# A sequence-DFT regrouped: four rows on one partition, odd halves turned by per-partition tangents, 95-column products

## The chip, the cores and the metric

The kernel runs on one core of a Trainium2 chip. The metric is the device time of one execution in microseconds (us). Every time in this study comes from an execution that was recorded as being in the fast state, at a mean granted TensorE clock of 0.99 or more. The kernel before takes 1940.77 us (median of three runs, 1940.24 to 1942.61).

Engine names as the profile uses them: PE is the matrix engine, PEld its weight loads, DVE the vector engine, ACT the scalar engine, POOL the GpSimd engine. SBUF is the large on-chip memory, PSUM the accumulator memory of PE.

## The reference

```python
# x: (8, 3008, 256); w_in: (256, 2048); w_out: (2048, 256); all float32
X = np.fft.fft(x, axis=1)              # along the sequence, 3008 points
X = np.fft.fft(X, axis=2)              # along the 256 channels
x = X.real.reshape(24064, 256)
h = x @ w_in
g = h * np.cos(h)
out = g @ w_out
```

The kernel doesn't transform the channels as such: the channel DFT is linear, so it is folded into `w_in` once. Because only the real part is wanted, one column of products serves two rows of the result, as a sum and as a difference (h_plus and h_minus), so 12032 columns are enough. What stays are two jobs. One is the "s-DFT", a 3008-point transform along the sequence for each of the 8 batches, which fills two rings of columns, `Rr` (real) and `Ir` (imaginary). The other is the dense part, 376 steps that read the rings.

## The kernel before

The program is one long list of events, each with a time in units of a step `T`. Each of the four busy engines works in the order of that list, so an event placed in a slot must be done before whatever follows it there. This is the dense step (lines joined and regrouped; `ACT`, `DVE`, `POOL` and `PE` added as remarks):

```python
for i in range(total):                 # total = 376 steps, 8 to a tile
    for dt, fn in (
        (-1.9, ext),                   # ACT: writes the 129th channel's share into the PSUM bank H
        (0.0, mm_P),                   # PE: H += Wc x Rr     (2 products of 256 columns)
        (0.9, dbl),                    # ACT: E = 2 H
        (2.17, mm_Q),                  # PE: H += Ws x Ir     (2 products)
        (3.55, h_minus),               # DVE: G[0:512] = E - H
        (4.2, k_plus), (4.8, k_minus), # ACT: round to integers
        (T + 0.2, r_plus), (T + 0.9, r_minus),     # DVE: H - round(H), in turns
        (T + 1.5, sin_plus), (T + 2.21, sin_minus),# ACT: the cosines
        (T + 2.2, g_plus), (T + 2.9, g_minus),     # DVE: h cos h
        (T + 2.91, sum_1), (T + 3.6, sum_3), (T + 4.4, sum_2), (2 * T + 0.3, sum_4),  # POOL
        (2 * T + 0.87, mm_X1), (2 * T + 3.04, mm_X2),  # PE: 7 products with w_out
    ): at(i * T + dt, ...)
```

Eleven products of 256 columns a step, two fp32 records each, keep PE busy. DVE has two gaps a step, after `h_minus` and after `r_minus`; POOL has one, after `sum_4`. Into these gaps goes the preparation of the next batch: POOL folds the loaded rows `xl` into even and odd halves (`e`, `o`), PE multiplies the halves with cosine and sine matrices `MC`, ACT and DVE unfold the result into the rings.

```python
class Dft:                             # one half transform (real or imaginary, even or odd k) of one batch
    def first_part(self):  self.mms(0, self.uv, False)    # for even k: 4 products of 189 or 190 columns
    def second_part(self): self.mms(1, self.pb, False)    # for even k: 3 products of 188 to 377 columns
    ...
def at_dft(step, gap, b, ri, kodd, stat):
    at(t + 2.905, lambda: d().clear())        # DVE: memset of a PSUM bank
    at(t + 4.75, lambda: d().first_part())    # PE
    at(t + T + 1.46, lambda: d().side())      # ACT
    at(u + 1.01, lambda: d().unfold())        # DVE
    at(u + 2.95, lambda: d().seed())          # ACT
    at(u + 4.75, lambda: d().second_part())   # PE
    at(u + T + 1.01, lambda: d().minus_sum()) # DVE, in0 from SBUF, in1 from PSUM
    at(u + T + 1.46, lambda: d().plus_sum())  # ACT
```

Each fp32 product gives two records in the trace. There are 33 such half transforms, 4 for each of 8 batches and one for a first channel column.

## Time and profile before

| | before |
|---|---|
| time | 1940.77 us (1940.24 to 1942.61) |
| span of the profiled run, mean granted clock | 1939.9 us, 0.999 |
| PE time lost against the widths of its products (own count) | 19.2 us |
| of that up to the first step / in steps 0 to 20 / later | 6.0 / 5.8 / 7.4 us |
| first step's products start | 36.3 us |
| s-DFT records, sum of their start-to-start spacings | 462, 95.3 us |

The profile's end of a matmul is modelled, so a busy share of 99% doesn't say that PE works without gaps. The own counts in this document go from the start of one PE record to the start of the next. A 256-column record, when nothing holds it, is 0.216 us after the one before; what exceeds the free spacing is called lost. For narrow and early records the free spacing is a choice, so another count differs by some us. (The Trainium skill, "Perfetto Trace Analysis", "Identifying the Most-Contended Engine", says the same of the matmul row: not a good measure, since pipelined instructions look smaller.)

The first table and the chain of waits, with three groups, from the page of the kernel before. A group's columns are line, engine, operation, output and input, shapes, count, then busy us and mean ns of one, then the engine's idle time just before it and what ended most of that.

```profile
PE 1921.9 (99%) x8878; PEld 1657.6 (85%) x8878; DVE 1426.7 (74%) x2387; ACT 1478.6 (76%) x2854; POOL 1412.0 (73%) x1926
...
PE 95%; DVE 2%; ACT 1%; issue 1%; DMA 1%; POOL 0%; SPq 0%; DVEq 0%; POOLq 0%
...
L293 POOL TENSOR_TENSOR G<-G 128x256 f32<-128x256 f32 x1500 | 1076.6, 728 | 491.8 <-DVE G L787 426.7
...
L284 PE MATMUL H<-Rr,Wc 128*128 128x256 f32 x1504 | 387.2, 380 | 0.7 <-ACT H L296 0.3
...
L284 PE MATMUL pB<-G,WT 128*128 128x256 f32 x752 | 224.0, 379 | 1.0 <-POOL G L293 1.0
```

PE is the bottleneck and hardly waits: 0.7 us in 1504 first products, 1.0 us for POOL's sums. The list of waits of the kernel before (us in all, times, longest):

```profile
POOL G L293 <- DVE G L787: 426.7, 333, 4.5
DVE G L787 <- ACT G L296: 256.4, 274, 4.2
...
ACT G L296 <- DVE G L290: 181.2, 357, 2.1
```

One step of the kernel before, from its timeline (start us, length us, what, how many; in brackets the idle time before). Only DVE's two first operations of the step and POOL are shown:

```profile
1011.15 3.02 POOL L293 TENSOR_TENSOR G<-G 128x256 f32<-128x256 f32 x4 [0.63 <-DVE G L787]
1011.52 0.68 DVE L290 TENSOR_TENSOR G<-E,H 128x512 f32<-128x512 f32 x1
...
1012.87 0.69 DVE L290 TENSOR_TENSOR G<-H,G 128x512 f32<-128x512 f32 x1 [0.66 <-ACT G L296]
...
1014.13 1.00 POOL L349 TENSOR_TENSOR e<-xl 128x381 f32<-128x381 f32 x1
```

Keep two things of it. POOL's four sums run without a break for 3.02 us, just where DVE has its gap, from 1012.2 (the end of `h_minus`, the `G<-E,H` line) to 1012.87. And `r_plus`, the `G<-H,G` line, starts 1.35 us after `h_minus`.

### The profile page before, as it was taken

To read this page: it belongs to the slowest core of one execution; us is meant where nothing else is said; L and a number is where in the kernel's file an instruction comes from. 1 tells how busy PE (TensorE), PEld (TensorE's weight loads), DVE (VectorE), ACT (ScalarE), POOL (GpSimd) and SP (SyncE) were. 2 spreads that over 40 slices of the span, in tenths; PEclk is the share of its full clock that TensorE was granted. 3 is DMA by queue.
4 is the path that set the end of the run, shared out by engine and by line. 5 is a ranking of instruction groups with operands and counts; after the bars stand their busy time and mean duration, and the time that the engine had idled before them with its cause. 6 is when DMAs were issued, how large, how long until landed. Compare 5 with 4: busy or idle time off the path is not lost.

```text
span 1939.9 us, 28429 instructions
## 1 busy us (share of the span) xinstructions
PE 1921.9 (99%) x8878; PEld 1657.6 (85%) x8878; DVE 1426.7 (74%) x2387; ACT 1478.6 (76%) x2854; POOL 1412.0 (73%) x1926
## 2 busy tenths in 40 slices
PE   8999999999999999999999999999999999999998
PEld 4888888888888888888888888888888888888887
DVE  5687777777777767777777777777767777677777
ACT  3777778877788777877778877787778777777786
POOL 6878768877687767877678776778768886555654
PEclk9999999999999999999999999999999999999999
DMA  9611210102101031110310103011030110000101
GB/s 274 35 29 17 61 47 20 18 14 71 33 20 18 11 78 31 18 20 9 87 27 13 22 7 94 13 21 26 7 84 15 24 27 7 17 12 12 21 10 25
DMA packets 258994, 67.59 MB, mean 35 GB/s; under 512 B 239970, under 2 KB 250858, under 8 KB 258842
## 3 DMA queue, kind: packets, MB, share of 16 engines
q1 hardware_dynamic: 251994, 50.81, 14.0%
q0 software_dynamic: 4672, 14.69, 2.6%
q8 instruction: 71, 1.16, 0.3%
q14 instruction: 81, 0.66, 0.1%
q10 hardware_dynamic: 2176, 0.26, 0.1%
HBM read 40.98 MB, written 24.69 MB: 34 GB/s over the span
## 4 chain that ended last, share of the span: by engine, by line
PE 95%; DVE 2%; ACT 1%; issue 1%; DMA 1%; POOL 0%; SPq 0%; DVEq 0%; POOLq 0%
PE H L284 38%; PE pC L284 17%; PE pD L284 16%; PE pB L284 16%; PE pA L284 8%; DMA w<-in_moe_w_in_dram 1%; DVE G L787 1%; ACT G L296 1%; DVE G L290 0%; ACT E L296 0%; DVE M L290 0%; DVE v L290 0%; DVE ab L290 0%; DVE ot L900 0%; DVE u L290 0%
## 5 line engine op out<-in xcount | busy, mean ns | idle before, releaser
L293 POOL TENSOR_TENSOR G<-G 128x256 f32<-128x256 f32 x1500 | 1076.6, 728 | 491.8 <-DVE G L787 426.7
L787 DVE SCALAR_TENSOR_TENSOR G<-H,G 128x512 f32<-128x512 f32 x376 | 259.2, 689 | 256.7 <-ACT G L296 256.4
L290 DVE TENSOR_TENSOR G<-H,G 128x512 f32<-128x512 f32 x376 | 260.0, 692 | 220.5 <-ACT G L296 217.5
L296 ACT ACTIVATE E<-H 128x512 f32<-128x512 f32 x376 | 224.4, 597 | 216.9 <-PE H L284 213.3
L284 PE MATMUL pC<-G,WT 128*128 128x256 f32 x1504 | 387.3, 379 | 2.1 <-DVE u L290 1.8
L284 PE MATMUL H<-Rr,Wc 128*128 128x256 f32 x1504 | 387.2, 380 | 0.7 <-ACT H L296 0.3
L284 PE MATMUL H<-Ir,Ws 127*128 127x256 f32 x1504 | 386.7, 378 | 0.7 <-ACT E L296 0.7
L296 ACT ACTIVATE H<-Rb,wex 128x256 f32<-128x256 f32 x752 | 360.6, 480 | 22.4 <-DVE G L787 8.1
L296 ACT ACTIVATE G<-H 128x512 int32<-128x512 f32 x376 | 224.5, 597 | 181.8 <-DVE G L290 180.6
L284 PEld LDWEIGHTS H<-Rr,Wc 128*128 128x128 f32 x1504 | 283.5, 190 | 48.5 <-ACT H L296 2.6
L284 PEld LDWEIGHTS pC<-G,WT 128*128 128x128 f32 x1504 | 283.7, 189 | 45.9 <-PE H L284 5.0
L284 PEld LDWEIGHTS H<-Ir,Ws 127*128 127x128 f32 x1504 | 284.7, 189 | 41.9 <-ACT E L296 1.4
L296 ACT ACTIVATE G<-G,halfpi 128x512 f32<-128x512 f32 x376 | 269.4, 717 | 0.6 <-DVE G L290 0.6
L290 DVE TENSOR_TENSOR M<-G,M 128x512 f32<-128x512 f32 x376 | 257.7, 685 | 0.0
L290 DVE TENSOR_TENSOR G<-E,H 128x512 f32<-128x512 f32 x376 | 255.5, 679 | 0.1
L787 DVE SCALAR_TENSOR_TENSOR G<-G,M 128x512 f32<-128x512 f32 x376 | 254.6, 677 | 0.6 <-ACT M L296 0.5
L296 ACT ACTIVATE M<-M,halfpi 128x512 f32<-128x512 f32 x376 | 246.1, 654 | 0.4 <-DVE M L290 0.3
L284 PE MATMUL pB<-G,WT 128*128 128x256 f32 x752 | 224.0, 379 | 1.0 <-POOL G L293 1.0
L296 ACT ACTIVATE M<-G 128x512 int32<-128x512 f32 x376 | 224.4, 597 | 0.0
L284 PE MATMUL pA<-G,w 128*128 128x256 f32 x752 | 223.8, 379 | 0.3 <-DVE G L787 0.3
L284 PE MATMUL pD<-G,WT 128*128 128x256 f32 x752 | 223.8, 379 | 0.0
L284 PE MATMUL pD<-G,w 128*128 128x256 f32 x752 | 223.7, 379 | 0.0
(147 smaller groups left out, 1886.6 us busy)
## 6 DMA issues: line engine op xcount, KB each, us to landing
out_dram<-ot SPq DMA_DIRECT2D x496, 32.0 KB
xl<-in_x_dram SPq DMA_DIRECT2D x32, 256.0 KB
out_dram<-ot SPq DMA_DIRECT2D x256, 2.0 KB
xl<-in_x_dram SPq DMA_DIRECT2D x31, 128.0 KB
Rb<-r SPq DMA_DIRECT2D x10, 376.0 KB
w<-in_moe_w_in_dram SPq DMA_DIRECT2D x4, 512.0 KB
w<-in_moe_w_out_dram SPq DMA_DIRECT2D x1, 2048.0 KB
MC<-dft_mats SPq DMA_DIRECT2D x2, 942.0 KB
```

The costliest lines, as they stand in the source:

```text
L284: nc.tensor.matmul(out_, lhsT=lhsT, rhs=rhs, start=start, stop=stop, skip_group_check=True)
L290: pin(nc.vector.tensor_tensor(out=o, in0=a, in1=b, op=op))
L293: pin(nc.gpsimd.tensor_tensor(out=o, in0=a, in1=b, op=op))
L296: pin(nc.scalar.activation(out=o, in_=i, func=func, **kw))
L787: nc.vector.scalar_tensor_tensor(out=o, in0=h, scalar=TWO_PI, in1=c, op0=ALU.mult, op1=ALU.mult)
```

## The change

Its intent is to cut PE's work in the s-DFT. Before, a half transform took its rows in six groups on up to 128 partitions and streamed 1514 or 1884 columns in 14 records through PE. Now rows s, 376-s, 376+s and 752-s lie on one partition (96 partitions, 8 slots), so that the cosine and sine sums can be split further, and a half transform needs 16 records of 94 or 95 columns. The price: for the odd halves, and with four steps each for a part of the even ones, the pairs of rows have to be turned by an angle that depends on the row. That is done in lifting steps, each `p + t q` with one tangent (or another constant) per partition from the table `RC`. The core of the diff, cut (`...`) and with comments added:

```diff
+    def stt(o, i, n, add):              # one turning step, on DVE, both inputs in SBUF
+        pin(nc.vector.scalar_tensor_tensor(
+                out=o, in0=i, scalar=RC[:, n : n + 1], in1=add, op0=ALU.mult, op1=ALU.add))
+    def turns0(z, ri):                  # 4 steps of 128 elements, for even k
...
+    def turns1(v, ri):                  # 16 steps, for odd k; both for real and imaginary: 40 a batch
...
     def dft_parts(ri, kodd, par):
-        ... four products of nh = 190 or 189, then two or three of up to 377 columns
+        ... four products of 95, 94, 95, 95 (or 95, 94, 95, 94) columns for each parity
...
+    def odd(self, down):                # the odd columns are now sums of two SBUF tiles, on DVE
+        for k0, step, n, a, b, op in sums(self.kodd):
+            ... vtt(self.ring[0:M, sl], u, v, op)
...
-        at(u + 1.01, lambda: d().unfold())
-        at(u + 2.95, lambda: d().seed())
+    def dve_room(n):                    # how much of a DVE gap may be filled, in us
+        return 0.0 if step % 8 in (...) else 0.64      # 0.72 in the first nine steps
+    def on_dve(n, cost, fn):            # next gap with room for cost
+    def dve_ns(elements):
+        return max(0.2, 0.08 + 1.04e-3 * elements)
+    def turn_all(n, ops, cost=0.19):    # a turning step is planned at 0.19 us
...
+    at(3 * T + 1.46, flip_ext)          # ACT: reads a slow load of the 129th channel
```

The folds on POOL go from 128 partitions x 381 elements to 96 x 508. The unfolding loses its two DVE passes and gets 16 such odd sums a batch instead.

## The prediction

> **What bounds it now.** The page's first table gives PE 99% (1921.9 of 1939.9 us), ACT 76%, DVE 74%, POOL 73%; the chain of waits is 95% PE. Matmul ends are modelled, so I counted start to start: the eleven 256-column products of a step run at 0.216 us a record, two records a product, without gaps. Against widths, PE loses some 19 us, 8 of them before 48 us and 4 more before 145 us; later there is next to no idle to recover. Only less PE work or a shorter prologue helps.
>
> **What PE sheds.** The s-DFT now is 462 records (14 of 188 to 377 columns a transform, 33 transforms). Their spacing follows columns (0.160 us at 190, 0.316 at 376); together 95.3 us. The change streams 758 or 756 columns a transform instead of 1514 or 1884, but in 16 records of about 95 columns: 528 records. By columns that would be 528 x 0.079 = 42 us. I don't believe it: the 16-column products that turn the extra channel, with 128-column weights, are spaced 0.118 us in the trace of before. So weight loading is the floor, and it doesn't shrink with 96 rows (those loads have 32). The Trainium skill, "TensorE: Matmul & The Clock Gate", LDWEIGHTS section, says that columns, not rows, set the load (128/1.2 = 107 ns); the trace's 118 agrees roughly. So 528 x 0.118 = 62 us: PE sheds about 33 us, not 53. The extra-channel work is about even.
>
> **What the others get.** POOL folds: before about 16 x 765 elements a batch at 2.35 ns (a 381-element piece takes 0.997 us), 36 us; after about 19,300 elements, 49 us: +80 us in all, to about 80%. DVE: 40 tangent turns and 16 odd sums a batch at 0.19 to 0.28 us, less the unfolds: +8 us a batch, to about 78%. ACT even. The new DVE ops read two SBUF operands. In the trace of before such an op (the v<-v,p sum) stretches an overlapping POOL fold from 0.997 to 1.46 us, as the skill's "SBUF — State Buffer", Terms, says of the shared port pair (the loser blocks). A fold piece also grows to about 1.3 us. The POOL sum that releases the pB product now ends a median 1.1 us early (5th percentile 0.5), so most of this hides; I allow 5 us of new PE stalls.
>
> **Prologue.** The first step's products start at 36.3 us. DVE folds of the first batch grow by a third (762 to 1016 elements, about 0.87 to 1.14 us), and halves and turns come before the first transform: it starts near 29 to 30 instead of 24.9 us. Given back: two odd folds become accumulating DMAs, and constants shrink by about 2.7 MB. Net +2 us.
>
> **Sum.** 1940.8 - 33 + 5 + 2 = about 1914 us (-1.4%). Range 1904 to 1930. Chances: faster by over 2% 0.11, within 2% 0.86, slower 0.03.
>
> **What would show it.** Spacing of the new records: 0.118 us (right), 0.08 (columns bind; then nearer 1895), or 0.16 and more. Sum of the s-DFT spacings about 62 us. First step's start at 37 to 41 us. PE's waits on POOL's and DVE's G in the list of waits: from about 2 us to 5 to 10. POOL near 80%, fold pieces often over 1.5 us where turns overlap.
>
> **What would make it wrong.** Narrow records cheaper than 0.118; POOL delayed past the 1.1 us margin in many steps (tenths of a us over 376 steps are tens of us); accumulating DMAs that land late and hold the first imaginary transform; PSUM banks held too long by the two-step transforms.

## The result, and the profile after

The changed kernel takes 2000.93 us (median of 4 runs, 1999.21 to 2002.8) against 1941.69 us (1940.24 to 1943.31) for the kernel before in the same rounds. Ratio 1.0305, 95% interval 1.0287 to 1.0323: slower by 3%. A ratio here is the mean time of one kernel's fast runs over that of the other's of the same rounds, so not quite the ratio of the medians that are quoted. The result is right (the output agrees with the reference).

The same lines of the page, for the changed kernel:

```profile
PE 1923.4 (96%) x8944; PEld 1627.1 (81%) x8944; DVE 1662.0 (83%) x2797; ACT 1486.4 (74%) x2861; POOL 1495.5 (75%) x1908
...
PE 70%; DVE 19%; ACT 4%; issue 3%; DMA 3%; SPq 1%; POOL 0%; DVEq 0%; POOLq 0%; ACTq 0%
...
L298 POOL TENSOR_TENSOR G<-G 128x256 f32<-128x256 f32 x1500 | 1082.5, 732 | 457.6 <-DVE G L796 355.3
L289 PE MATMUL H<-Rr,Wc 128*128 128x256 f32 x1504 | 395.4, 385 | 23.1 <-ACT H L301 23.1
...
L289 PE MATMUL pB<-G,WT 128*128 128x256 f32 x752 | 230.2, 388 | 6.0 <-POOL G L298 4.8
```

PE's busy time even rose by 1.5 us. That is the trap of the modelled ends: start to start, the s-DFT fell from 95.3 us in 462 records to 63.1 us in 528 (the page's count of PE goes up by the same 66), and PE's lost time rose from 19.2 to 106.7 us. Those two, -32.2 and +87.5, give +55.3 us, which is nearly the whole difference of the spans, 1997.4 - 1939.9 = 57.5 us. A recount that takes the median spacing of each shape as free gives 24.8 and 118.5 us lost (+93.7), and 94.3 and 58.9 us for the s-DFT when nothing holds it (-35.4), +58.3 us together. So some 4 of the 63.1 us are stalls inside the s-DFT.

DVE is the engine that grew: +235 us, where I had expected some 65 (8 a batch), and its share of the chain went from 2% to 19%. Its new groups, with shapes kept apart (turning steps of two tiles, then one of the odd sums):

```profile
L423 DVE SCALAR_TENSOR_TENSOR e<-e,RC 96x128 f32<-96x128 f32 x128 | 74.5, 629 | 0.0
L423 DVE SCALAR_TENSOR_TENSOR o<-o,RC 96x127 f32<-96x127 f32 x128 | 71.7, 607 | 0.0
...
L295 DVE TENSOR_TENSOR Ir<-sb 127x188 f32<-127x188 f32 x14 | 10.3, 774 | 0.0
```

A turning step of 128 elements takes 0.61 to 0.63 us on average, not the 0.19 that the change plans with. Where POOL isn't running it takes 0.34 us (own selection from the trace); four in a row, while POOL computes nothing, take 1.13 us, 0.28 each. So the 0.19 was too little even without POOL, and the larger part of the excess is what happens beside POOL. In all, 344 steps that read `RC` take 209.6 us and 152 odd sums 87.6 us.

The waits that grew in the changed kernel's list:

```profile
POOL G L298 <- DVE G L796: 355.3, 309, 4.5
ACT G L301 <- DVE G L295: 284.8, 445, 2.2
...
PEld pB L289 <- POOL G L298: 26.7, 60, 2.3
...
PE H L289 <- ACT H L301: 23.1, 27, 7.7
...
PE H L289 <- DVE H L556: 12.6, 11, 1.4
...
ACT x L301 <- DMA x<-in_x_dram: 10.3, 1, 10.3
```

ACT waits 104 us more for DVE's `G`; PE now waits for ACT's write of H, for DVE's clearing of the DFT bank and for POOL's sums. The timeline of a step in which a real odd half is turned shows how that starts:

```profile
1020.62 3.03 POOL L298 TENSOR_TENSOR G<-G 128x256 f32<-128x256 f32 x4 [0.55 <-DVE G L796]
...
1020.99 0.68 DVE L295 TENSOR_TENSOR G<-E,H 128x512 f32<-128x512 f32 x1
...
1021.58 2.21 DVE L423 SCALAR_TENSOR_TENSOR e<-e,RC 96x128 f32<-96x128 f32 x3
...
1023.72 0.68 DVE L295 TENSOR_TENSOR G<-H,G 128x512 f32<-128x512 f32 x1
...
1024.43 0.72 ACT L301 ACTIVATE G<-G,halfpi 128x512 f32<-128x512 f32 x1 [0.95 <-DVE G L295]
```

Three turning steps, planned at 0.57 us, take 2.21 us, as long as three of POOL's sums, and the last ends 0.14 us after POOL's last sum (1023.79 and 1023.65). `r_plus` comes 2.73 us after `h_minus` instead of 1.35, and ACT sits idle for it. `h_minus` itself runs in its usual 0.68 us in the middle of POOL's sums: it has one input in PSUM. Over the whole trace, a turning step that starts while a POOL sum is running ends 0.147 us (median) after the end of that sum; one that comes just as a sum starts takes 0.88 us, that is 0.73 + 0.15. Of the 320 steps of 127 or 128 elements, 209 take more than 0.4 us (0.78 on average). The reverse is rare: 8 steps began 0.04 to 0.08 us before a sum; they kept their 0.33 to 0.34 us, and the sum took 0.84 to 0.89 us instead of 0.73.

At the start there are two more losses. The chain of waits of the changed kernel up to 75 us contains a load that lands at 71.5 us:

```profile
32.15 39.31 DMA x<-in_x_dram
...
71.55 0.13 ACT x L301
```

ACT works in order and waited there 10.3 us (the last of the waits above), in step 3 of 376; from step 3's first products to step 4's, PE took 14.7 us (59.6 to 74.3) instead of 4.75. And the first products start later, by the timelines of before (first two lines) and after:

```profile
24.90 1.56 PE L284 MATMUL pA<-MC,e 128*128 128x190 f32 x8
...
36.34 1.13 PE L284 MATMUL H<-Rr,Wc 128*128 128x256 f32 x4 [0.26 <-issue]
```

```profile
31.42 0.68 PE L289 MATMUL pA<-MC,e 95*128 95x95 f32 x4 [0.76 <-DVE e L362]
...
43.49 1.13 PE L289 MATMUL H<-Rr,Wc 128*128 128x256 f32 x4 [1.74 <-ACT H L301]
```

### The profile page after: what moved, and what is told of

Same layout as the page of the kernel before. It is cut to its first block, busy times and chain, and to the rows that moved or that the text cites. A ratio compares the mean times of both kernels' runs of the same rounds, so it can differ in the third digit from the quotient of the medians.

```text
span 1997.4 us, 28934 instructions
## 1 busy us (share of the span) xinstructions
PE 1923.4 (96%) x8944; PEld 1627.1 (81%) x8944; DVE 1662.0 (83%) x2797; ACT 1486.4 (74%) x2861; POOL 1495.5 (75%) x1908
## 4 chain that ended last, share of the span: by engine, by line
PE 70%; DVE 19%; ACT 4%; issue 3%; DMA 3%; SPq 1%; POOL 0%; DVEq 0%; POOLq 0%; ACTq 0%
PE H L289 27%; PE pB L289 12%; PE pC L289 12%; PE pD L289 12%; PE pA L289 6%; DVE G L295 5%; DVE G L796 4%; DVE M L295 2%; ACT G L301 2%; DMA x<-in_x_dram 2%; DVE o L423 2%; DVE e L423 2%; DVE v L295 1%; DMA xl<-in_x_dram 1%; ACT M L301 1%
## 5 line engine op out<-in xcount | busy, mean ns | idle before, releaser
L289 PE MATMUL H<-Rr,Wc 128*128 128x256 f32 x1504 | 395.4, 385 | 23.1 <-ACT H L301 23.1
L289 PEld LDWEIGHTS H<-Rr,Wc 128*128 128x128 f32 x1504 | 277.0, 191 | 74.5 <-ACT H L301 37.7
L289 PE MATMUL pB<-G,WT 128*128 128x256 f32 x752 | 230.2, 388 | 6.0 <-POOL G L298 4.8
L289 PE MATMUL pB<-G,w 128*128 128x256 f32 x752 | 225.1, 381 | 0.3 <-DVE u L295 0.2
```

The source lines that it names most:

```text
L289: nc.tensor.matmul(out_, lhsT=lhsT, rhs=rhs, start=start, stop=stop, skip_group_check=True)
```

## The experiments

The theory after the first look: DVE's new operations have two inputs in SBUF, and such an operation has to wait for the POOL operation that is running. (The Trainium skill has the lock: "SBUF — State Buffer", Terms, on the shared port pair, "the loser **fully blocks**, it doesn't share bandwidth", and "GPSIMD Engine Reference", Specifications, lists the conflict with DVE instructions that have two SBUF inputs.) The rivals: the mere number and time of the new DVE operations; the one slow load; the longer start; too many banks taken by the two-part transforms. The last two have no run of their own; e2 leaves the banks as they are.

Seven kernels were run, each timed in 4 runs.

### e1: the read of the slow load put three steps later

```diff
-    at(3 * T + 1.46, flip_ext)
+    at(6 * T + 1.46, flip_ext)
```

> The changed kernel with one edit: the ACT copy that flips the extra channel's rows is issued at step 6, not step 3. Theory A (ACT executes in order and sits 10.3 us behind the slow one-channel load, so steps 3 to 4 take 14.7 us): the wait of ACT on the x load goes to under 1 us, the step from 3 to 4 falls to about 5 us, time about 1990 us (10 less than 2001). Rival: the stall in the first 100 us is DVE work that only moves elsewhere: time within 3 us of 2001.

Measured: 1990.93 us (1989.31 to 1994.38), ratio 1.0248 (1.0231 to 1.0265); right result. So this edit takes back 10 of the 59 us. From step 3's first products to step 4's, PE now takes 6.7 us (own reading of the trace), a little more than the 5 expected. Its list of waits no longer has the load; ACT's wait for DVE stays on top:

```profile
ACT G L301 <- DVE G L295: 288.1, 445, 2.2
```

The slow load is a real, separate cause, and the smaller one.

### e2: the wide turning steps replaced by operations with one input (wrong result)

```diff
     def stt(o, i, n, add):
+        if o.shape[1] >= 127:
+            pin(nc.vector.transpose(out=o[:, 0:96], in_=i[:, 0:96]))
+            return
```

As many DVE operations, in the same places, writing the same tiles (96 columns of them), but each reading one. The 24 narrow turning steps of the 129th channel stay.

> The changed kernel with wrong results on purpose: every tangent turn of 127 or 128 columns becomes a 32-block transpose of 96 columns of its first operand on DVE, so the same number of DVE instructions in the same places, but one SBUF input instead of two. Theory L (a two-SBUF-input DVE op cannot start while POOL executes one; it waits for POOL's op to end, 0.73 us for a sum): turns fall from a mean of 0.6 us to about 0.25 us, DVE busy falls by some 100 us, PE stalls of 106 us are about halved, time 1940 to 1970 us. Rival C (the count and place of inserted DVE instructions is what delays the chain): time stays within 5 us of 2001. Rival P (POOL's longer fold pieces delay its sums): stays within 10 us of 2001.

Measured: 1953.27 us (1948.11 to 1955.75), ratio 1.0048 (1.0031 to 1.0065), relative error 1.12 as intended. 48 us are gone. Its first table and the group that took the turning steps' place:

```profile
PE 1903.4 (97%) x8944; PEld 1636.6 (84%) x8944; DVE 1550.4 (79%) x2797; ACT 1486.7 (76%) x2861; POOL 1493.9 (76%) x1908
```

```profile
L423 DVE STREAM_TRANSPOSE e<-e 96x96 f32<-96x96 f32 x128 | 25.5, 244 | 0.0
```

The number of operations is not the cause, and neither is the number of banks, which is the same here. But their time changed together with their inputs, 0.24 us against 0.62, and the data flow isn't the real one. So the next pair puts the same question to the other kernel.

### b1 and b2: the same DVE traffic in the kernel before, with two inputs and with one

Both add 360 operations whose result nobody reads, in bursts of three every third step, at the place in the step where the change puts its turning steps. The sources are constants.

```diff
+    for i in range(10, total - 8, 3):
+        for _ in range(3):
+            at(i * T + 4.25, lambda: vtt(sd, CC[0:96, 0:128], CC[0:96, 128:256], ALU.add))      # b1
+            at(i * T + 4.25, lambda: pin(nc.vector.transpose(out=sd, in_=CC[0:96, 0:128])))     # b2
```

> The kernel before, with 360 idle-value DVE additions of 96x128 of two SBUF operands into a scratch tile, three in a burst after the h_minus of every third step, where POOL is in its sums. Theory L: each takes about 0.6 to 0.9 us instead of 0.25, a burst takes about 2.2 us in an idle window of 0.66 us, and the time rises by 40 to 150 us. Rival C: the rise is the same as for the one-input control below.

> Control to the one above: the same 360 places, but 32-block transposes of 96x128 with one SBUF operand. Theory L: each takes about 0.25 to 0.3 us, the time rises by under 8 us. Rival C: the same rise as with pairs.

Measured: b1 2007.69 us (2004.69 to 2008.17), ratio 1.0332 (1.0315 to 1.0349); b2 1950.8 us (1949.52 to 1953.04), ratio 1.0047 (1.003 to 1.0063). Both give the right result. The added tile's operations, b1 and then b2 (least, median and greatest ns):

```profile
L291 DVE TENSOR_TENSOR sd<-CC x360: 271/769/1119, 95.1 to 1955.8; 96x128 f32<-96x128 f32 x180
```

```profile
L1200 DVE STREAM_TRANSPOSE sd<-CC x360: 288/307/310, 94.8 to 1897.1; 96x128 f32<-96x128 f32 x180
```

Without any part of the change, small operations with two SBUF inputs cost the kernel 65 us, and those with one input 8 to 9 us (the expectation had said under 8). The smallest b1 operation, 0.271 us, is shorter than the smallest b2 one, so it isn't the work in the operation. It is what the operation waits for after it has started: the record of its length contains that wait. POOL's busy time is the same in all three kernels (1412.0, 1412.5 and 1412.8 us), so it isn't POOL's operations that get longer.

### f1: the turning steps with one operand in PSUM, right result

If the second SBUF input is what hurts, the same arithmetic with one operand in PSUM must be cheap. ACT copies the first operands of a group of steps into a free PSUM bank; this was done for 232 of the 320 wide turning steps (the odd ones from the third batch on, the even ones from the fourth). The earlier ones keep their SBUF operands. The flip stays late as in e1, the order of the folds was adapted to the banks, some steps moved to other DVE gaps, and the middle row's work comes ten steps later.

```diff
+    def stage_copy(box, v, rng):        # ACT
+        ps = bank("H")
+        box["v"] = ps[...]
+        act(box["v"], v[:, rng[0] : rng[1]])
...
-    stt(v[:, o], v[:, i], c, v[:, a])
+    stt(v[:, o], box["v"][:, i - r], c, v[:, a])
```

> A correct version of the changed kernel. The flip is issued at step 6 as in e1_flip_late, and 232 of the 320 wide turns (odd ones from batch 2, even ones from batch 3) take their first operand from a PSUM bank to which ACT has copied it, so they have one SBUF input; folds and banks are re-ordered for the bank's sake, and the middle row's work comes ten steps later. Theory L: these turns fall from about 0.6 us to 0.35 us or less although every one is still an addition of two tensors, and the time falls from 1991 (e1) to 1950 to 1965 us. Rival C (instruction count and places): stays at 1985 to 2000, since ACT even gets some 50 copies more. If the one-input test helped because a transpose does less arithmetic, this stays there too.

Measured: 1953.66 us (1952.17 to 1955.87), ratio 1.0066 (1.0049 to 1.0082), right result. Both kinds of turning step in this one run, with the operand `H` from PSUM and without:

```profile
L423 DVE SCALAR_TENSOR_TENSOR e<-H,RC,e 96x128 f32<-96x128 f32 x96 | 29.5, 338 | 1.9 <-ACT H L301 1.0
...
L423 DVE SCALAR_TENSOR_TENSOR e<-e,RC 96x128 f32<-96x128 f32 x32 | 17.3, 587 | 0.0
```

Same instruction, same shape, same run: 0.338 us against 0.587. Against e1, whose edit it contains, it wins 37 us (1990.93 to 1953.66; the two ran in different jobs, and the ratios, 1.0248 and 1.0066, say 35). It pays for that with 56 copies on ACT. The two durations show the effect of the operand; how much of the 35 to 37 us is due to it, and how much to the new order, this run doesn't separate.

### f2: f1, and most odd sums with one operand in PSUM

```diff
+        def odd_psum(self, s, n):
+                act(box["ps"][:, 0:m], self.sb[:, c0 : self.n])
+                act(box["ps"][:, 256 : 256 + m], self.ab[:, c0 : self.n])
...                 # then vtt(ring, SBUF half, PSUM half, op), from the fourth batch on where time allows
```

> As f1_psum_turns, and from batch 3 on most sums of the odd columns also take their second operand from a PSUM copy (ACT copies of 95 or 189 columns). Theory L: another 5 to 15 us less than f1, so 1938 to 1958 us; about equal to the kernel before. Rival: the extra ACT copies and PSUM banks cost what the shorter waits give: within 3 us of f1.

Measured: 1951.3 us (1947.86 to 1953.82), ratio 1.0045 (1.0029 to 1.0062), right result. Its interval overlaps f1's, so a gain over f1 is not shown: the theory's 5 to 15 us were missed, and the rival (within 3 us of f1) fits. The odd sums did get shorter: 84 of them with a PSUM operand take 0.29 to 0.32 us on average, those without mostly 0.5 to 0.6 (own count). They are worth far less than the turning steps here.

What is left in f2 lies at its start, by the times at which steps 0, 20, 100 and 375 begin on PE (own reading of the traces):

| kernel | step 0 at, us | steps 0 to 20 | steps 20 to 100 | steps 100 to 375 |
|---|---|---|---|---|
| before | 36.3 | 106.7 | 403.4 | 1375.3 |
| changed | 43.5 | 127.4 | 408.9 | 1399.7 |
| e1 | 45.6 | 121.0 | 408.7 | 1399.4 |
| e2 | 39.9 | 136.2 | 397.2 | 1362.8 |
| f1 | 42.9 | 119.3 | 402.8 | 1368.4 |
| f2 | 45.5 | 121.0 | 402.7 | 1364.4 |
| e3 (below) | 40.2 | 118.7 | 396.8 | 1362.7 |

From step 100 on, f2 is 10.9 us faster than the kernel before, so there the s-DFT's saving arrives in part: its records after step 100 sum to 57.5 us before and 37.2 in f2, 20.3 less (own count). Before step 100 it loses 22.7 us (569.2 against 546.5 at step 100). One piece of that is four sums for the 129th channel in a single DVE gap, planned at some 0.11 us each, and PE's wait for the bank behind them. From f2's timeline:

```profile
146.34 3.37 DVE L362 TENSOR_TENSOR xe<-xe 96x160 f32<-96x160 f32 x4
...
153.38 1.73 PE L289 MATMUL H<-MC,xe 95*40 95x95 f32 x16 [2.42 <-DVE H L729]
```

Such gaps come back a second time. In e1's trace, after a gap of PE, the records run at double spacing for some 3.4 us (at 54, 94 and 155 us). The Trainium skill, "TensorE: Matmul & The Clock Gate", Part 1, describes a gate that looks at windows of about 3.4 us and halves the clock after an idle one; these traces agree in the length and in the factor (the profile's own record of the granted clock shows 0.5 from 53.3 and 94.3 us on for 3.4 us each, and from 152.3 us on for 6.8). The mean granted clock fell from 0.999 to 0.993 in the changed kernel.

### e3: both causes taken away at once (e2 and e1 together, wrong result)

```diff
     def stt(o, i, n, add):
+        if o.shape[1] >= 127:
+            pin(nc.vector.transpose(out=o[:, 0:96], in_=i[:, 0:96]))
+            return
...
-    at(3 * T + 1.46, flip_ext)
+    at(6 * T + 1.46, flip_ext)
```

> One-input turns (wrong result on purpose, as in e2) together with the later flip_ext (as in e1). Theory: the two losses are separate, so this is e2's 1953.3 us less the 10 us that the later flip saved alone: 1941 to 1946 us, within 0.3% of the kernel before; the wait for the one-channel load disappears from ACT's waits. What is then still lost against the prediction's 1914 us is the longer prologue, the odd sums and the early steps, about 30 us. Rival 1: the flip's stall hides behind other early losses once the turns are cheap, or the other way round (the same early slack pays for both): 1950 us or more. Rival 2: the early losses feed on one another: under 1938 us.

Measured: 1937.15 us (1935.25 to 1938.51), ratio 0.9972 (0.9956 to 0.9989). The theory's 1941 to 1946 is missed on the low side, and the number falls where the second rival had put it: the two causes were not simply additive. The later flip saved 10 us alone and 16 us on top of e2. The list of waits of e2 suggests why:

```profile
ACT x L301 <- DMA x<-in_x_dram: 18.9, 1, 18.9
```

With cheap turning steps the kernel came to the read of the load sooner (step 0 at 39.9 us instead of 43.5), while the load landed later than in the run of the changed kernel (77.6 against 71.5 us), so ACT stood there for 18.9 us instead of 10.3. Removing the stall thus saves more.

e3 and e1 differ only in the turning steps, so their lists of waits test the way from DVE to PE. PE's wait for ACT's write of H falls from 15.3 to 4.5 us, its wait for DVE's clearing of the DFT bank from 12.6 us to nothing that the list shows, and the waits of its loads on POOL's sums from 24.6 to 14.3 us.

With both gone, the change is worth 0.3%, about 5 us. That is less than the 2% that would count as faster, and it is a kernel with a wrong result. No version with the right result that I ran beats the kernel before; f2 comes nearest, 0.45% behind it.

## Why the prediction was wrong

The prediction was 1914 us, range 1904 to 1930, with slower by over 2% at 0.03. It came out at 2000.93 us, slower by 3%. Term by term:

- "PE sheds about 33 us": right. 95.3 us became 63.1, a saving of 32.2 us. The spacing of the narrow records is 0.109 to 0.112 us, a little under the 0.118 that I took from the products of the extra channel in the trace of before. So it was right not to scale by columns (0.079). The changed kernel's own trace has the control: its 32 extra-channel records with 94 or 95 columns but loads of 40 columns instead of 128 are spaced 0.082 us. That the sum came within 1 us of 62 is partly luck: without stalls it is 58.9 us, and some 4 us of stalls make up the rest. The LDWEIGHTS section of "TensorE: Matmul & The Clock Gate" gives 128/1.2 = 107 ns for a load of 128 columns, whatever the rows; this case, with 94 or 95 rows, agrees to 2 to 5 ns.
- "POOL folds: +80 us in all": right. POOL's busy time rose from 1412.0 to 1495.5 us, and a fold piece took 1.30 us on average, as expected. The sums' mean barely moved (728 to 732 ns).
- "DVE: 40 tangent turns and 16 odd sums a batch at 0.19 to 0.28 us": this is the step that failed. They measured 0.61 us and 0.58 us on average. The range was right for a step that meets no POOL operation (0.28 us in a row, 0.34 alone); what it left out is the wait. I had named the shared port pair and its rule, and even looked up an example of it. In that example, POOL's fold was the one that stretched (0.997 to 1.46 us), and so I booked the conflict as a cost to POOL, which had slack. But the one that starts second waits, whichever it is. POOL's four sums run back to back through one of DVE's two gaps, and the folds run in the other, so the turning steps mostly came second: 209 of the 320 wide ones were lengthened, where 8 got in before a sum and lengthened it. DVE's busy time rose by 235 us instead of some 65. Runs e2, b1 with b2, and f1 show it in three ways that don't share their weak points: other operations in the changed kernel, the two kinds of traffic in the kernel before, and the same arithmetic with a PSUM operand.
- "I allow 5 us of new PE stalls": it was 87.5 us in all. The allowance came from POOL's margin of 1.1 us a step. The way to PE is another: turning steps of 2.2 us in a gap of 0.7 delay `r_plus`, that delays ACT's cosines, ACT's writes to H and everything after it. I had no margin for that chain in the sum at all. (The waits of e1 and e3 above show it: it shrinks with the turning steps.) The bound of an engine that is off the critical path isn't its busy share (I wrote 78%) but the room in the gap where the new work goes.
- "Prologue +2 us": the first step came 7.1 us later. By the trace, DVE's folds of the first batch run in a nearly unbroken row from 20.4 to 40 us, with four halving operations and turns of 0.28 us each where I took 0.19, after a wait of 1.87 us for a load of `xl`. This is only read from the trace. The kernels whose turns are the same there start at 42.9 to 45.6 us; e2 and e3 start at 39.9 and 40.2 us, within the predicted 37 to 41. Their shorter turns explain only some 0.8 us of that: in e2 that load also let DVE go on 1.8 us sooner (18.65 against 20.43 us). A run made to test it doesn't exist.
- The slow load of the 129th channel is nowhere in the prediction. It cost 10 us. The line that reads it, on an engine that works in order, stands in the diff. The trace of before shows no wait for this load: its reader there, a copy on POOL, runs only at 81.3 us. The change put the read some 20 us earlier, before the load had landed.
- "POOL delayed past the 1.1 us margin in many steps" stood among the ways to be wrong. It is half right: the waits of PE's loads on POOL did grow (from 1.9 to 26.7 us). With one-input turns (e2) 12.8 us of them stay. So about half came from DVE's lateness; the rest isn't explained by a run.

What remains of the distance to 1914 when both shown causes are away? e3 stands at 1937, 23 us above. Its lost PE time, by the same count as before, is 6.3 us up to the first step, 21.2 in steps 0 to 20 and 19.7 later, 47.2 in all, where the kernel before has 19.2. With the saving of 32.2 us that makes 1940.8 - 32.2 + 28.0 = 1936.6 us, so the sum closes to a few us (with e3's own s-DFT records, 60.5 us in all, it gives 1934.0): the loss is in the early steps (15.4 us more) and spread over the later ones (12.3 us more). Which share of it belongs to the folds on DVE, to the odd sums, to the sums of the 129th channel and to the halved clock after gaps is open. I tried to spread the 129th channel's work over more gaps at honest costs, but that schedule pushed the second batch past the steps at which its columns are due, and it couldn't be built without a deadlock. It was never run.

## What to carry to other kernels

Before you move work to an engine with idle time, take the gap it goes into and ask which other engine is running there, and whether the new operation and that engine's share a lock; here a small operation with two SBUF inputs in a row of POOL operations took as long as the POOL operation it met (0.73 + 0.15 us instead of 0.34). A lock has two losers: cost it once with either engine coming second. If the operation has to be there, give it one operand in PSUM, and plan its slot with the length that the trace shows, not with its element count.

## What the Trainium skill lacked or had wrong

- "SBUF — State Buffer" states the lock rightly, and the runs agree with it. It lacks the length of the loser's delay when DVE is the loser: here the DVE operation ended 0.147 us (median) after the POOL operation it met. It also lacks a warning that a row of small DVE operations alternates with a row of POOL operations one for one: three steps of 128 elements took 2.21 us beside three POOL sums of 0.73 us each.
- "SBUF — State Buffer" advises to schedule whichever is off the critical path. A way out follows from its section "Who interferes with whom", which says that a DVE instruction with at most one SBUF input doesn't contend; the page doesn't draw the step that run f1 measured, to copy one of the two operands to PSUM first (0.338 us against 0.587 for the same instruction in the same run), nor its price (56 copies on ACT).
- "GPSIMD Engine Reference" lists the conflict, without a number. In the kernel before, 360 added DVE operations with two SBUF inputs cost 65 us, and 360 with one input 8 to 9 us, with POOL's busy time unchanged.
- "TensorE: Matmul & The Clock Gate": its load formula held, at 0.109 to 0.112 us for 107 ns.
- "Perfetto Trace Analysis" warns of the matmul busy share. PE's busy time rose by 1.5 us while its s-DFT work fell by 32.2 us and its lost time rose by 87.5 us.
